# The keys' weight scale ahead of the second row tile's preparation, seven warming products fewer, and two stretches of the execution order rewritten

## The chip, the cores and the metric

The kernel runs on one core of one Trainium2 chip. The metric is the device time of one execution in microseconds (us), as the median of several runs. In what follows PE is TensorE, DVE is VectorE, ACT is ScalarE, POOL is GpSimd and SP is SyncE, the engine that issues nearly all transfers here.

## What is computed

```python
def _A_ref(x, wqkv, wo):                       # linear attention, 32 heads of 16
    qkv = (x @ wqkv).reshape(B, S, 3, H, Dh).transpose(2, 0, 3, 1, 4)
    q, k, v = qkv[0], qkv[1], qkv[2]
    phi = lambda t: where(t > 0, t + 1, exp(t)) + 1e-6
    pq, pk = phi(q), phi(k)
    kv = einsum("bhsd,bhse->bhde", pk, v);  z = einsum("bhsd->bhd", pk)
    num = einsum("bhqd,bhde->bhqe", pq, kv)
    den = einsum("bhqd,bhd->bhq", pq, z)[..., None] + 1e-6
    return (num / den).transpose(0, 2, 1, 3).reshape(B, S, D) @ wo
def _B_ref(x, w1, w3, w2):                     # SwiGLU
    return (silu(x @ w1) * (x @ w3)) @ w2

x = A_x                                        # 2048 rows of 512
for layer in range(2):                         # the same weights in both layers
    x = x + _A_ref(layernorm(x), wqkv, wo)
    x = x + _B_ref(layernorm(x), w1, w3, w2)   # inner width 1792
```

All is float32; one sequence of S = 2048 rows, D = 512.

## The kernel before

**Tiling.** The rows stand as 16 tiles of 128 (t = 0 to 15), D as four pieces of 128 (k). Each float32 matrix is split into a high and a low float16 part, and a product is made in three passes (high by high, low by high, high by low). Weights are scaled by a power of two ahead of the split, so that their largest value lies where float16 is finest.

**Stages.** Attention of layer 0 is plain (`attention`), tile by tile: keys, then queries, then output. The SwiGLU blocks and the attention of layer 1 (`attention7`) use a scheme with seven products instead of eight for pairs of halves; there the projections of queries and keys land in banks called qa, qb, qc, ka, kb, kc, and the SwiGLU's in ba, bb, bc. `po` is the bank of an output product.

**The lead-in** (lines 2328 to 2408). SP issues loads: x's first tile, four pieces of the keys' weights (`att_piece`), more tiles of x (`x_piece`, L2317), and blocks of the SwiGLU weights (`load_block`, L960, 896 KB each, b0, b1 and so on). For a tile of x, DVE takes the layer norm's moments (L907, L908), POOL makes scale and offset of them (L915 to L919), ACT normalises (L922). Tiles 0 and 1 are then turned on PE (`first_tile`): ACT rounds to the high half (L2356), POOL subtracts for the low half (L2358), PE multiplies four pieces of each half with an identity matrix (L2352, bank `turn`), ACT copies the turned halves out (L2354). Later tiles are turned by a transposing DMA (L937, L1856), with the split by L857 or L859 and L1855 before it.

In the same time the keys' weights are scaled and split: DVE takes the largest absolute value of each piece (L787), then of the four (L803), PE turns this column into a row (L806, bank `pm_k`), DVE takes the largest again (L808) and makes the scale (L809 to L819), and then ACT writes the high parts (L834) and DVE the low parts (L835), piece by piece. `keep_busy` (L2366) issues products of ones that nobody reads, so that PE works while it waits: 22 at the start and 10 behind `pm_k`.

**The key stage.** Tile by tile: twelve products `pk` on PE (L945), the positive map phi on ACT (L1337 to L1339) and DVE (L1348), the split of the result on ACT (L1394) and DVE (L1403), and then twelve products into `gt` (L945, four banks, the function `gram`), which use that split, two tiles behind.

**The order.** The program is emitted in the order of the Python code, and then `arrange` (L676) pins another order on each of the five engines: the table `ORDER` (L72 to L474) lists, for each engine, the instructions by their number in the order of emission, and each is chained behind the one ahead of it in the list. So an instruction can stand anywhere on its engine, as far as data and buffers allow, and what stands behind a waiting instruction waits too. Which piece of x or which block is issued when is decided by SP's list, not by the place of the call in the code. DVE's, ACT's and POOL's lists decide the same for the statistics, evictions and splits.

**The second layer's attention** runs at about 567 to 805 us of the profile. Query products land in qb, qc and qa; ACT empties them (L1632) or DVE does (L1636), and a bank is filled again only when it is empty. L1715, L1716, L1730 to L1751 and L1757, L1758 weigh the queries and divide; L1951 adds the output to x, POOL makes the next layer norm's scale (L1969, L1970), ACT normalises (L922) and splits (L1986), POOL subtracts (L1992), and the halves are turned by DMA.

Of the kernel before, what the change touches and what calls it, by code (L numbers as in the profile page):

```python
# [9 lines left out]
F32 = mybir.dt.float32  # L10
# [483 lines left out]
def kernel(  # L494
# [1833 lines left out]

    x_piece(0, 1)
    att_piece(1)  # L2330
    x_piece(1, 4)
    for item in LOADS[0].split():
        what, t = item.split(":")
        i = int(what[1:] or 0)
# [121 lines left out]
```

## Time and profile before

| | |
|---|---|
| median of 3 runs | 1139.43 us (1138.91 to 1141.31) |
| profiled execution, device time | 1139.86 us |
| span of its instructions | 1138.1 us |
| PE busy | 1125.6 us, 9124 products |
| DVE, ACT, POOL busy | 855.4, 661.2, 426.7 us |
| granted PE clock, mean of the span | 1.000 |
| data moved by DMA | 162.94 MB, mean 143 GB/s |

Times of events count from the span's start. A busy time of PE counts each product up to its modelled end, so products that run back to back overlap: a product of 512 columns has a busy time of 0.38 us, and the next one starts before it ends. Idle times of PE in the profile's brackets are therefore a little shorter than the distance of the starts tells.

### The profile page before, as it was taken

How to read it: one execution, taken by the hardware profiler on the slowest of the kernel's cores; microseconds unless marked ns; L12 is line 12 of the kernel's file. 1: busy time of each engine (PE TensorE's matmuls, PEld its weight loads, DVE VectorE, ACT ScalarE, POOL GpSimd, SP SyncE). 2: the span in 40 equal slices, each digit the busy share in tenths (PEclk: the TensorE clock that was granted, in tenths of full speed). 3: DMA queues.
4: the chain of work that ended last, by engine and by line, in shares of the span. 5: the costliest groups of instructions: out<-in, count | busy, mean ns of one | idle time of the engine just before them, and what ended most of it. 6: DMA issues, size and time to landing. Idle time of an engine off the chain costs nothing.

```text
span 1138.1 us, 22474 instructions
## 1 busy us (share of the span) xinstructions
PE 1125.6 (99%) x9124; PEld 888.9 (78%) x9124; DVE 855.4 (75%) x1468; ACT 661.2 (58%) x1104; POOL 426.7 (37%) x477
## 2 busy tenths in 40 slices
PE   8999999999999999999999999999999999999998
PEld 3445445888888888888886676578888888888887
DVE  6799878996978887889896488857855666465556
ACT  7678778765644455455578666586544434343442
POOL 5831697402001222344668416871152210302113
PEclk9999999999999999999999999999999999999999
DMA  8995765678573332241358955573372440220001
GB/s 255 281 305 182 175 139 111 146 224 239 171 257 141 117 149 102 92 174 66 80 130 187 267 207 124 112 170 69 98 215 87 178 190 1 84 84 29 11 20 56
DMA packets 171768, 162.94 MB, mean 143 GB/s; under 512 B 139536, under 2 KB 147984, under 8 KB 167056
## 3 DMA queue, kind: packets, MB, share of 16 engines
q1 hardware_dynamic: 171664, 161.51, 48.7%
q8 instruction: 71, 1.16, 0.4%
q14 instruction: 33, 0.27, 0.1%
HBM read 80.08 MB, written 47.32 MB: 112 GB/s over the span
## 4 chain that ended last, share of the span: by engine, by line
PE 90%; DVE 4%; POOL 3%; ACT 2%; DMA 1%; issue 1%; SPq 0%; POOLq 0%; ACTq 0%; DVEq 0%
PE bb L945 24%; PE po L2095 20%; PE bc L945 12%; PE gt L945 7%; PE ba L945 6%; PE po L945 4%; PE po L2115 3%; PE pq L945 3%; PE pk L945 3%; PE kb L945 2%; PE qb L945 1%; PE kc L945 1%; PE qc L945 1%; DMA arena<-in_A_x_dram 1%; DVE arena L869 1%
## 5 line engine op out<-in xcount | busy, mean ns | idle before, releaser
L945 PEld LDWEIGHTS <-arena 128*128 128x128 f16 x6648 | 646.1, 98 | 208.2 <-issue 7.3
L945 PE MATMUL bb<-arena 128*128 128x256 f16 x2688 | 350.1, 273 | 0.0
L2095 PE MATMUL po<-arena 128*128 128x256 f16 x2058 | 288.1, 273 | 0.0
L2050 ACT ACTIVATE arena<-bb 128x512 f32<-128x512 f32 x196 | 115.4, 594 | 200.3 <-PE bb L945 165.5
L2095 PEld LDWEIGHTS <-arena 128*128 128x128 f16 x2058 | 201.3, 98 | 23.5
L945 PE MATMUL bc<-arena 128*128 128x256 f16 x1344 | 179.5, 273 | 1.2 <-DVE arena L1951 1.1
L2053 DVE TENSOR_TENSOR arena<-arena,bc 128x512 f32<-128x512 f32 x112 | 76.6, 684 | 82.7 <-PE bc L945 48.6
L2005 ACT ACTIVATE arena<-arena,scalars 128x512 f32<-128x512 f32 x112 | 74.6, 666 | 88.9 <-DVE arena L2053 67.3
L2144 DVE SCALAR_TENSOR_TENSOR arena<-po,scalars,arena 128x256 f32<-128x256 f32 (+1 forms) x180 | 101.2, 584 | 31.1 <-PE po L2095 21.8
L2011 DVE TENSOR_TENSOR arena<-arena 128x1280 f16<-128x1280 f32 (+1 forms) x90 | 106.5, 1187 | 20.5 <-ACT arena L2009 20.2
L2009 ACT ACTIVATE arena<-arena 128x512 f16<-128x512 f32 (+1 forms) x112 | 101.1, 904 | 33.5 <-DVE arena L2024 13.4
L2006 DVE SCALAR_TENSOR_TENSOR arena<-arena,scalars 128x512 f32<-128x512 f32 x112 | 78.7, 706 | 38.1 <-ACT arena L2005 38.0
L945 PE MATMUL ba<-arena 128*128 128x256 f16 x672 | 91.8, 273 | 0.2 <-DVE arena L2006 0.2
L945 PE MATMUL gt<-arena 128*128 128x512 f16 x384 | 90.5, 379 | 1.3 <-DVE arena L1403 1.3
L945 PE MATMUL po<-arena 128*128 128x512 f16 x384 | 86.7, 379 | 1.6 <-DMA arena<-arena 1.6
L2011 POOL TENSOR_TENSOR arena<-arena 128x512 f16<-128x512 f32 x22 | 27.0, 1228 | 118.3 <-ACT arena L2009 111.3
L2153 POOL TENSOR_TENSOR arena<-arena 128x512 f32<-128x512 f32 x27 | 36.9, 1365 | 84.4 <-DVE arena L2144 84.4
L2152 POOL TENSOR_TENSOR arena<-arena 128x512 f32<-128x512 f32 x27 | 38.1, 1411 | 71.2 <-DVE arena L2144 69.1
L869 DVE SCALAR_TENSOR_TENSOR arena<-arena,scalars 128x512 f16<-128x512 f32 (+2 forms) x74 | 57.5, 792 | 2.5 <-ACT arena L867 2.4
L922 ACT ACTIVATE arena<-arena,nb_all,rs_all 128x512 f32<-128x512 f32 x64 | 50.6, 804 | 14.9 <-POOL nb_all L919 7.8
L2021 POOL TENSOR_TENSOR arena<-arena 128x256 f32<-128x256 f32 x10 | 7.8, 777 | 131.0 <-DVE arena L2006 131.0
L867 ACT ACTIVATE arena<-arena,scalars 128x512 f16<-128x512 f32 (+2 forms) x74 | 51.5, 717 | 6.2 <-DVE scalars L819 1.7
(234 smaller groups left out, 1458.1 us busy)
## 6 DMA issues: line engine op xcount, KB each, us to landing
arena<-xb_d SPq DMA_DIRECT2D x12, 1792.0 KB, 7.2
xb_d<-arena SPq DMA_DIRECT2D x8, 1792.0 KB, 7.4
w_d<-arena SPq DMA_DIRECT2D x5, 1792.0 KB, 7.7
arena<-w_d SPq DMA_DIRECT2D x5, 1792.0 KB, 8.0
arena<-in_B_w_dram SPq DMA_DIRECT2D x8, 896.0 KB, 7.0
arena<-in_B_w_dram SPq DMA_DIRECT2D x28, 256.0 KB, 3.0
xt_d<-arena SPq DMA_DIRECT2D x8, 896.0 KB, 4.5
arena<-xt_d SPq DMA_DIRECT2D x8, 896.0 KB, 5.4
```

What stands on the lines that cost most here:

```text
L867: nc.scalar.activation(hi, src, AF.Copy, scale=scale)
L869: lambda: nc.vector.scalar_tensor_tensor(lo, src, scale, hi, OP.mult, OP.subtract)
L922: nc.scalar.activation(dst, x_sb[:, t, :], AF.Identity, scale=rs_all[:, t : t + 1], bias=nb_all[:, t : t + 1],)
L945: nc.tensor.matmul(dst, lhs(a, k), rhs(b, k), start=first and k == 0 and i == 0, stop=last and k == n - 1 and i == len(PASSES) - 1, skip_g ...
L2005: nc.scalar.activation(t, gate, AF.Silu, scale=info["u1"])
L2006: nc.vector.scalar_tensor_tensor(t, up, info["hid"], t, OP.mult, OP.mult)
L2009: nc.scalar.activation(hs[:, 0, lo:hi], t[:, lo:hi], AF.Copy)
L2011: engine.tensor_tensor(hs[:, 1, lo:hi], t[:, lo:hi], hs[:, 0, lo:hi], OP.subtract)
L2050: nc.scalar.activation(dst, bank_, AF.Copy)
L2053: nc.vector.tensor_tensor(dst, dst, bank_, OP.add)
L2095: nc.tensor.matmul(po[:, i * HALF : (i + 1) * HALF], hs[:, a, qx, cs], w2[:, b, qw, :], start=g == ends[0] and i + a + b == 0, stop=g == e ...
L2144: nc.vector.scalar_tensor_tensor(dst, src, cb, to, OP.mult, OP.add)
```

## The change

The code of the lead-in is emitted in another order. Before: warming, statistics of tiles 0 and 1 (with two L787 and tile 0's preparation among them), tile 1's preparation, the weight scale (with tile 2's statistics and ten warming products inside), the split. After: warming, statistics of tile 0, all four L787, tile 0's preparation, the weight scale (with tile 1's statistics and three warming products inside), then tile 1's preparation, tile 2's statistics, the split. Since the pinned lists decide what runs when, this shifts the numbers in the lists; the lists themselves decide the rest.

```diff
-    x_piece(1, 4)
+    x_piece(1, 2)
+    x_piece(2, 4)
...
-    keep_busy(22)
-    ln_stats(0, 1)
-    parts = small.tile([P, NK], F32, tag="parts", name="parts")
-    ln_stats(1, 1)
-    abs_max(parts[:, 0:1], st_att[1][:, 0, :])
-    abs_max(parts[:, 1:2], st_att[1][:, 1, :])
-    first_tile(0)
-    for k in (2, 3):
-        abs_max(parts[:, k : k + 1], st_att[1][:, k, :])
-    first_tile(1)
-    issue_loads(1)
-    for i, _ in enumerate(weight_scale("k", parts, 2.0**14)):
-        if i == 0:
-            ln_stats(2, 1)
-        if i == 1:
-            keep_busy(10)
-    m, e, scale = info["k"]
...
+    if True:
+        keep_busy(22)
+        ln_stats(0, 1)
+        parts = small.tile([P, NK], F32, tag="parts", name="parts")
+        for k in range(NK):
+            abs_max(parts[:, k : k + 1], st_att[1][:, k, :])
+        first_tile(0)
+        for i, _ in enumerate(weight_scale("k", parts, 2.0**14)):
+            if i == 0:
+                ln_stats(1, 1)
+            if i == 1:
+                keep_busy(3)
+        first_tile(1)
+        issue_loads(1)
+        ln_stats(2, 1)
+        m, e, scale = info["k"]
...
```

The rest of that part (split, further factors, tile 2's preparation, tile 3's statistics) is the same, and `if True:` does nothing. The lists of `ORDER` are exchanged for others. Renumbered to the emission before, they are equal except in two stretches: from the start to about 128 us of the profile before, and from about 567 to 805 us. SP's list has the same numbering before and after; its beginning:

```diff
     "SP": (
-        "0 5-6 1 3 2 4 7 9-10 20 19 17 16 23 18 21 8 24 28 22 25 15 34 26 52 29 36 40 53 32 30 27 "
-        "39 41 35 33 43 57 42 11 48 47 37 31 50 38 46 51 55 45 44 71 56 58 49 59 14 60 54 61 65 "
...
+        "0 6 5 3 1 4 2 7 10 9 15 8 24 19 17 16 20 28 18 21-23 25 34 26 53 40 29 11 52 32-33 30 36 "
+        "27 39 41-42 35 47-48 57 46 51 37-38 50 43 55 45 58 56 44 59 31 49 61 60 65 54 63-64 62 "
...
```

Here 0, 5, 6, 7, 10, 9, 15, 8, 24, 19 and 28 are pieces of x (tiles 0, 1, 2, 3, 5, 4, 10, 7, 8, 6 and 9), 1 to 4 the keys' weights, 20 is the block b0, 31 and 49 the blocks b3 and b4, 54 and 65 two blocks more, 11 to 14 pieces of the values' weights and such, 60 and 63 the transposes of tiles 12 and 13.

What the lists say in names, for the places where the prediction looks (t0, t1, t2 are row tiles):

```
           before                                    after
SP         x0 x1 x2, keys' weights, x3               x0 x2 x1, keys' weights, x3
DVE        moments t0 t1 t2, 4 x L787, L803          moments t0 t1 t2, 4 x L787 (0,3,2,1), L803
POOL       identity; scale t0 t1 t2; L2358 t0, t1    scale t0; identity; scale t1 t2; L2358 t0, t1
ACT        cast of identity; L922 L2356 t0, t1;      L922 L2356 t0; L922 t1; cast of identity;
           L922 t2; copies t0; L935 t2; L834         L2356 t1; L922 L935 t2; copies t0; L834
           x 4; copies t1 high, low                  x 4; copies t1 low, high
PE         21 warm; turn t0 high, low, t1 high,      21 warm; turn t0 high and low by turns;
           low; one warm; pm_k; 10 warm; pk          pm_k; turn t1, with 4 warm among it; pk
ACT, 702   L1715, L1632 qc, L1632 qb, L922 x 2,      L1715, L1632 qc, L1632 qb, L1632 qb,
           L1986, L1632 qb, ...                      L922 x 2, L1986, ...
PE, 702    po t8, qb, qc, qb, qc, (the qb at         qb, qc, qb, po t8, qb, qc, (the qb at
           708.50), qb, qa, qb, qc, po               708.50), po, qa, qb, qb, po
```

SP's x pieces of tiles 10, 7 and 8 stand ahead of the block b0 after and behind the first transposes before; the block b3 stands directly ahead of b4 after, and some fifteen places earlier before. In the second stretch the loading of an activation table (in front of L1834) stands behind an L1757 at 730 us, and at 746 us before; some groups of `kb` products change places between 598 and 660 us.

More of the change, by code (lines that the diff above doesn't have):

```diff
@@ L2372, in keep_busy @@
             )
-    keep_busy(22)
-    ln_stats(0, 1)
-    parts = small.tile([P, NK], F32, tag="parts", name="parts")
-    ln_stats(1, 1)
-    abs_max(parts[:, 0:1], st_att[1][:, 0, :])
-    abs_max(parts[:, 1:2], st_att[1][:, 1, :])
-    first_tile(0)
-    for k in (2, 3):
-        abs_max(parts[:, k : k + 1], st_att[1][:, k, :])
-    first_tile(1)
-    issue_loads(1)
-    for i, _ in enumerate(weight_scale("k", parts, 2.0**14)):
-        if i == 0:
-            ln_stats(2, 1)
-        if i == 1:
-            keep_busy(10)
-    m, e, scale = info["k"]
-    for k in range(NK):
-        split(wk_s[:, 0, k, :], wk_s[:, 1, k, :], st_att[1][:, k, :], scale)
-    info["uk"] = scaled(e, 2.0**-23)
-    info["nuk"] = scaled(info["uk"], -1.0)
-    b = scalar()
-    nc.vector.tensor_scalar(b, m, float(D), 2.0, op0=OP.mult, op1=OP.add)
-    low_pow2(b, b)
-    nc.vector.reciprocal(b, b)
-    info["tk"] = scaled(b, 2.0**14)
-    info["itk"] = scalar()
-    nc.vector.reciprocal(info["itk"], info["tk"])
-    first_tile(2)
-    ln_stats(3, 1)
+    if True:
[14 more added lines that the diff above has]
+        m, e, scale = info["k"]
+        for k in range(NK):
+            split(wk_s[:, 0, k, :], wk_s[:, 1, k, :], st_att[1][:, k, :], scale)
+        info["uk"] = scaled(e, 2.0**-23)
+        info["nuk"] = scaled(info["uk"], -1.0)
+        b = scalar()
+        nc.vector.tensor_scalar(b, m, float(D), 2.0, op0=OP.mult, op1=OP.add)
+        low_pow2(b, b)
+        nc.vector.reciprocal(b, b)
+        info["tk"] = scaled(b, 2.0**14)
+        info["itk"] = scalar()
+        nc.vector.reciprocal(info["itk"], info["tk"])
+        first_tile(2)
+        ln_stats(3, 1)
     for t in range(3):
```

725 rows, old and new, of the table ORDER are left out of this document.

## The prediction

> **What bounds the kernel now.** I read the page first: busy times, slices, chain.
>
> ```profile
> PE 1125.6 (99%) x9124; PEld 888.9 (78%) x9124; DVE 855.4 (75%) x1468; ACT 661.2 (58%) x1104; POOL 426.7 (37%) x477
> ...
> PEclk9999999999999999999999999999999999999999
> ...
> PE 90%; DVE 4%; POOL 3%; ACT 2%; DMA 1%; issue 1%; SPq 0%; POOLq 0%; ACTq 0%; DVEq 0%
> ```
>
> TensorE (PE) works 1125.6 of 1138.1 us at full clock, and 90% of the chain is its products. No edit can bring more than the 12.5 us in which it stands, plus products left out. So the next view is that of the waits, for PE:
>
> ```profile
> PE turn L2352 <- POOL arena L2358: 2.0, 2, 1.4
> ...
> PE po L945 <- DMA arena<-arena: 1.6, 2, 0.8
> ...
> PE gt L945 <- DVE arena L1403: 1.3, 2, 0.7
> ...
> PE qb L945 <- ACT arena L1632: 1.0, 1, 1.0
> ```
>
> The columns are total, times and longest. Two waits lie in the lead-in (turn), two in the key stage of the first layer (gt); qb and po lie in the second layer's attention. All four are in the places where the change works; the question is which of them go, and what is late next. For that I went through the timeline of each place and set the old and the new hand-written order side by side.
>
> **The lead-in.** The rows of the timeline, up to the first key product:
>
> ```profile
> 1.11 6.70 PE L2366 MATMUL warm<-ones 128*128 128x512 f16 x21 [1.11 <-DVE ones L708]
> ...
> 4.32 0.66 DVE L907 BATCH_NORM_STATS2 st<-arena 128x6 f32<-128x512 f32 x1
> ...
> 5.83 0.69 DVE L907 BATCH_NORM_STATS2 st<-arena 128x6 f32<-128x512 f32 x1 [0.64 <-DMA arena<-in_A_x_dram]
> ...
> 6.66 2.68 DVE L787 TENSOR_REDUCE parts<-arena 128x1 f32<-128x512 f32 x4
> ...
> 6.90 0.19 POOL L915 TENSOR_SCALAR ve<-mv_all 128x1 f32<-128x1 f32 x1
> ...
> 8.23 2.27 POOL L2358 TENSOR_TENSOR arena<-arena 128x512 f16<-128x512 f32 x2
> ...
> 9.38 0.16 DVE L803 TENSOR_REDUCE scalars<-parts 128x1 f32<-128x4 f32 x1
> ...
> 9.44 0.51 PE L2352 MATMUL turn<-arena 128*128 128x128 f16 x6 [1.41 <-POOL arena L2358]
> ...
> 11.06 0.44 PE L806 MATMUL pm_k<-arena,scalars 128*128 128x128 f32 x2
> ...
> 11.34 2.32 PE L2366 MATMUL warm<-ones 128*128 128x512 f16 x10
> ...
> 13.19 2.74 DVE L835 SCALAR_TENSOR_TENSOR arena<-arena,scalars 128x512 f16<-128x512 f32 x4
> ...
> 13.55 0.81 PE L945 MATMUL pk<-arena 128*128 128x512 f16 x3
> ```
>
> The seven products that go would be 7 x 0.216 = 1.5 us (the ten take 2.32 us, of which the last one's own length, 0.38 by the page, so (2.32 - 0.38)/9 = 0.216 from start to start). But they are not what the first key products (pk) wait for in the end. Those need the four low parts of the keys' weights, which DVE writes from 13.19 to 15.93; the twelve products of tile 0 from 13.55 are done at 13.55 + 12 x 0.216 = 16.14. So the last of them starts just as the last low part is there. Without the seven, the products start earlier and wait in between. The price of the removal is nothing and so is its gain, unless the low parts come earlier. Do they?
>
> They hang on the scale: largest value (L787, L803), the turn on PE (pm_k), L808, exponent, split. The change gives x's third tile the second load, and on DVE the statistics of tile 1 still stand ahead of the four L787. Tile 1's statistics ran at 4.32, from the second transfer; now they need the third, which landed at 5.83. Then DVE does tile 1 and 2 in a row: 5.83 + two times about 0.8, so the four L787 start at about 7.5 and L803 ends at about 10.3 instead of 9.54. On POOL the scales of tiles 1 and 2 (each some 1.35 us, 6.90 to 8.23 in the rows) now both stand ahead of the first L2358: it starts at about 9.4 instead of 8.23, ends at 10.6, and PE gets its next product to turn at about 10.65 instead of 9.44. pm_k stands behind these turned products, eight of 0.06, so at 11.05 to 11.15: as before. ACT's two copies of tile 0's turned halves, which then stand right ahead of its high parts, end some 0.1 later than these began before (12.43). The low parts thus end at 15.95 to 16.05. Behind them ACT copies tile 1's turned halves in exchanged order (needed first, done last): another 0.1 to 0.3. Lead-in: +0.3 us, between 0 and +0.5; not the -1.5 that the count of products suggests.
>
> What the change opens is a gap on PE: the identity matrix that every turned product needs is built behind tile 0's scale on POOL and cast behind tile 1's normalising on ACT, so it is there at about 9.3 and not at 2.5. That itself delays nothing, for the low half comes at 10.6. But from 7.65, the end of the warming, to 10.65 PE has one product of 0.06: 2.9 us of standing, where before it stood 1.6 and then 0.8. The trace has only the other end: 21 warming products take 6.70 us, that is 11 x 0.216 + 10 x 0.43, so half speed for 4.3 us at the start, and after the gaps of 1.6 and 0.8 the ten run at 0.216. So 2.9 us of idling is between what was harmless and what is unseen. [...] No row of before shows a gap of this length. Its price is a rival below.
>
> **The key stage, 14 to 114 us.**
>
> ```profile
> 25.57 1.05 SPq L2317 DMA_DIRECT2D arena<-in_A_x_dram  x2
> ...
> 26.45 0.69 DVE L907 BATCH_NORM_STATS2 st<-arena 128x6 f32<-128x512 f32 x1 [1.31 <-DMA arena<-in_A_x_dram]
> ...
> 27.06 0.74 DVE L1403 SCALAR_TENSOR_TENSOR arena<-arena,scalars 128x512 f16<-128x512 f32 x1
> ...
> 27.85 2.32 PE L945 MATMUL gt<-arena 128*128 128x512 f16 x10 [0.71 <-DVE arena L1403]
> ...
> 40.21 0.68 DVE L907 BATCH_NORM_STATS2 st<-arena 128x6 f32<-128x512 f32 x1
> ...
> 40.82 0.73 DVE L1403 SCALAR_TENSOR_TENSOR arena<-arena,scalars 128x512 f16<-128x512 f32 x1
> ...
> 41.60 3.61 PE L945 MATMUL gt<-arena 128*128 128x512 f16 x16 [0.64 <-DVE arena L1403]
> ```
>
> The first gt wait: L1403 stood on DVE behind statistics that waited 1.31 us for a piece of x. In the new order of SP the x pieces 7, 8 and 10 are issued right after 5 and 4, some 15 to 20 us earlier, ahead of the weight block b0, and DVE does their statistics by about 24. Then the L1403 of tile 1 runs at about 26.5 and the stall goes: 0.87 us (product starts 0.216 apart; the last before it at 26.77). The second: L1403 of tile 3 and 4 come out at about 35.7 and 39.8 by the new order, wanted at 37.3 and 41.8; 0.80 us goes. Sum -1.67. I followed pk and gt so up to tile 9: slack 0.8 to 1.7 us each time, so nothing of DVE, ACT or POOL is late next.
>
> What is late next could be a transpose. The window table and SP's row:
>
> ```profile
> 60.00:80.00 20.00, 20.00 (x96) 9.46 (x95) 18.19 (x34) 14.58 (x24) 6.47 (x10) 1.00 1.12 316
> ...
> 80.00:100.00 20.00, 20.00 (x95) 9.56 (x94) 19.56 (x45) 15.45 (x27) 0.56 (x4) 1.00 0.49 148
> ...
> 47.79 0.44 SPq L960 DMA_DIRECT2D arena<-in_B_w_dram  x1
> ...
> 62.92 2.09 SPq L1856 DMA_TRANSPOSE arena<-arena  x1
> ...
> 68.27 3.93 SPq L1856 DMA_TRANSPOSE arena<-arena  x1
> ...
> DMA to landing us min/median/max: 7.1/7.1/7.1
> ...
> 72.04 2.75 PE L945 MATMUL pk<-arena 128*128 128x512 f16 x12
> ```
>
> (In the first two rows the last columns are DMA share and GB/s, and the fifth is DVE's busy time; the landing row is that of the transpose issued at 62.92.) From 60 to 80 the transfers are full: share 1.12. Tile 12's transpose, issued at 62.92, landed at 70.0, and its pk began at 72.04. The change moves the block b3 (896 KB, issued at 47.79) to just before b4, close ahead of this transpose, and takes a 256 KB piece out from in front. PE wants tile 12 at about 69.5. If the DMA stays as full in 45 to 60, the backlog ahead of the transpose is no larger and it lands before that: no cost. If the time that b3 leaves is not filled, 0.9 MB at 316 GB/s, 2.9 us, comes on top of 70.0: 3.4 us of stall. The earlier issue (tile 12's preparation moves with PE) takes some 1.5 off. I take +0.3, nearer the first, since the wo pieces and stores move into that place; the ends are 0 and 3.4. From 80 to 100 DVE is busy 19.56 of 20: work that the new order pushes out of the earlier stretch finds 0.44 us there. The stalls at 114.4 and later begin from PE's own ends and shift with it.
>
> **The second layer's attention, 567 to 805 us.**
>
> ```profile
> 702.08 1.13 ACT L1715 ACTIVATE arena<-arena,scalars 128x1024 f32<-128x1024 f32 x1
> ...
> 705.82 1.52 ACT L922 ACTIVATE arena<-arena,nb_all,rs_all 128x512 f32<-128x512 f32 x2 [1.71 <-POOL nb_all L1970]
> ...
> 707.91 0.55 ACT L1632 ACTIVATE arena<-qb,ones,scalars 128x256 f32<-128x256 f32 x1
> ...
> 708.50 1.47 PE L945 MATMUL qb<-arena 128*128 128x256 f16 x12 [0.99 <-ACT arena L1632]
> ...
> 733.18 4.32 POOL arena L1992 x3
> ...
> 742.55 4.08 DMA arena<-arena
> ...
> 746.67 2.76 PE L945 MATMUL po<-arena 128*128 128x512 f16 x12 [0.83 <-DMA arena<-arena]
> ```
>
> At 708.50 PE waits for a bank that ACT's L1632 empties at 707.91. That L1632 stands behind two L922, and these behind POOL (ACT idles 1.71). The new order puts it ahead of them, into the idle time. The stall (1.15 us) and two small ones behind it (0.16, 0.18) go: -1.5. In exchange PE's qc group now comes before the eviction behind L1715 (702.08 to 703.2): about +0.9 there by hand, part of which the moved qb and po products take. PE is then some 0.5 ahead at 715. The chain that decides at 746.67 (DVE L1636, L1716, POOL L1758, L1992 x3, transposes, po) starts from qb evictions that come about 1.1 earlier, so both po stalls (736.56 and 746.67) stay and what is behind them moves by -1.15. The kb products moved at 598 to 660 meet six stalls of 0.13 to 0.20: -0.3 (0 to -0.5). The load of an activation table, moved from 746 to 730 on ACT, falls into idle time there; uncovered it costs 1.3. Stretch: -1.45, between 0 and -2.3.
>
> **Sum.** 0.3 - 1.67 + 0.3 - 1.45 = -2.5 us against the profiled execution's 1139.86: 1137.3. The median of the runs (1139.43) lies 0.43 below that execution, so 1136.9. A measurement here tells 0.2% from nothing, 2.28 us: the forecast lies just beyond that bound.
>
> **Rivals.**
>
> 1. Transposes late, slower. Tile 12's lands 3.4 late, and tile 13's (issued at 68.27 before, now also behind b5 and another block) 1.5 to 2; DVE, full from 80, can't give it back. +0.3 - 1.67 + 5.2 - 1.45 = +2.4: 1141.8. It decides from the point at which tile 12 lands after 72: then its stall alone (2.5) outweighs what the stage gained. For it: the share of 1.12. Against: the bytes ahead of the transpose are fewer by 256 KB. Chance 0.22.
> 2. The clock falls in the 2.9 us gap. Then some 4.3 us of products at half speed follow, ten of 512 columns, 0.21 more each: +2.1, sum -0.4: 1139.0. For it: fewer products behind the gap. Against: gaps of 1.6 and 0.8 did nothing. Chance 0.08.
> 3. The warming products did hold pk (ten end at 13.66, pk begins at 13.55): lead-in -1.5 instead of +0.3, sum -4.3: 1135.1. Against: the low parts' end at 15.93. Chance 0.10.
> 4. The second stretch does nothing: the wait at qc and a longer one at 746.67 take all of it: sum -1.1: 1138.3. For it: both po stalls hang on transposes and POOL, not on PE. Chance 0.10.
>
> **The numbers.** The forecast has 0.50. Around it the spread is some 1.5 us, from the ends of the two unsure terms: 0.32 of it is faster by over 0.2%, 0.16 within, 0.02 slower. Rival 1 gives 0.20 slower and 0.02 within; rival 2 0.05 within, 0.01 faster, 0.02 slower; rival 3 0.10 faster; rival 4 0.10 within. Faster 0.43, within 0.2% 0.33, slower 0.24. Range 1134.4 to 1142.0: below it lies about a tenth (rival 3 with a good second stretch), above it about a tenth (rival 1 with more than its price).
>
> **What would show it.** Right: tile 0's last pk ends at 16.2 to 16.5, the pm_k product runs near 11.1, the gt waits for L1403 are gone, no qb wait for L1632 near 708, po still waits for transposes near 735 and 745. Wrong: a pk that waits for a DMA between 65 and 82 (rival 1); products of 512 columns 0.43 apart after 10.6 (rival 2); a tile 0 done before 15 (rival 3); the po wait of 0.83 grown to 2 (rival 4).

## The result, and the profile after

| | before | changed |
|---|---|---|
| median of 22 runs each | 1139.93 us | 1137.41 us |
| profiled execution, and its span | 1139.86, 1138.1 us | 1137.83, 1136.1 us |
| products on PE | 9124 | 9117 |
| mean granted clock of the profiled execution | 1.000 | 0.998 |

The ratio is 0.9977, 95% interval 0.9970 to 0.9983: faster by 2.5 us. The forecast was 1136.9 us within 1134.4 to 1142.0, a gain of 2.5. The total came out as forecast; the terms for the lead-in and for the second stretch did not, and two waits that the sum left out went as well.

In what follows, line numbers of the changed kernel stand one or two higher than before (L2366 is L2368, L945 is L946, L1632 is L1633). First the view of PE's waits, after:

```profile
PE turn L2354 <- ACT arena L705: 1.7, 1, 1.7
PE qb L946 <- ACT arena L1633: 1.3, 1, 1.3
PE turn L2354 <- POOL arena L2360: 1.2, 1, 1.2
...
PE kc L946 <- DMA arena<-arena: 0.4, 1, 0.4
PE turn L2354 <- DVE scalars L809: 0.4, 1, 0.4
PE qc L946 <- ACT arena L1633: 0.3, 1, 0.3
```

Both gt waits for L1403 are gone, and both po waits. The turn waits have become longer (2.9 us, and 0.4 more, instead of 2.0), a qb wait for the same line is there at another place, and kc and qc wait where they did not. Counted from start to start of its products, PE stands (or runs at half clock) for 13.8 us before and 13.3 after; with the seven products that is the 2.0 us of the spans.

Since both programs issue the same products behind the lead-in, the start of the n-th product from the end can be set against that of the same n in the trace of before. The difference (minus: ahead of before) at several places, in us, worked out from the traces of single executions:

| time in the trace of before | 24 | 45 | 128 | 230 to 560 | 640 | 700 | 780 to the end |
|---|---|---|---|---|---|---|---|
| changed | +1.11 | -0.55 | -0.85 | -1.18 | -0.52 | -0.48 | -2.02 |
| first stretch alone | +0.68 | -0.99 | -1.28 | -1.61 | -1.17 | -1.19 | -1.98 |
| second stretch alone | +0.24 | +0.37 | +0.37 | +0.36 | +0.40 | +0.45 | -0.51 |
| gap filled | -0.03 | -1.03 | -1.32 | -1.65 | -1.42 | -1.37 | -2.58 |
| ten warming products | +1.94 | +0.28 | -0.02 | -0.34 | -0.20 | -0.15 | -0.68 |
| before, three warming products | +0.01 | -0.09 | -0.08 | -0.07 | +0.26 | +0.25 | -0.59 |
| before, x early | +1.90 | +0.23 | +0.24 | +0.24 | +0.39 | +0.39 | +0.14 |
| x's tile 1 second | -0.57 | -1.59 | -1.88 | -2.20 | -1.52 | -1.47 | -2.99 |
| qb first | +0.42 | -1.24 | -1.54 | -1.86 | -1.20 | -1.16 | -2.38 |
| gap filled, block behind | +0.18 | -0.30 | -0.60 | -0.92 | -0.88 | -0.75 | -1.84 |
| gap filled, block behind, x's tile 1 second | -0.28 | -1.94 | -2.24 | -2.56 | -2.51 | -2.45 | -3.76 |
| changed, once more | +1.63 | -0.04 | -0.33 | -0.66 | +0.99 | +1.03 | -0.46 |
| gap filled, once more | -0.11 | -1.77 | -2.07 | -2.39 | -2.19 | -2.14 | -3.64 |

The first row is the result in short: the lead-in costs 1.11, the first stretch gives back 2.29, the second brings another 0.84. The other rows are the experiments below. A second trace of the changed kernel has +1.63, -2.29 and +0.20 in the same places: the first stretch repeats, the other two differ from execution to execution.

The lead-in after, PE and DVE from the timeline:

```profile
5.94 0.70 DVE L908 BATCH_NORM_STATS2 st<-arena 128x6 f32<-128x512 f32 x1 [1.72 <-DMA arena<-in_A_x_dram]
...
7.57 2.49 DVE L788 TENSOR_REDUCE parts<-arena 128x1 f32<-128x512 f32 x4
...
9.29 0.22 PE L2354 MATMUL turn<-arena 128*128 128x128 f16 x1 [1.69 <-ACT arena L705]
...
10.68 0.56 PE L2354 MATMUL turn<-arena 128*128 128x128 f16 x7 [1.17 <-POOL arena L2360]
...
11.08 0.44 PE L807 MATMUL pm_k<-arena,scalars 128*128 128x128 f32 x2
...
12.60 1.06 PE L2368 MATMUL warm<-ones 128*128 128x512 f16 x2
...
13.20 2.74 DVE L836 SCALAR_TENSOR_TENSOR arena<-arena,scalars 128x512 f16<-128x512 f32 x4
...
14.41 2.84 PE L946 MATMUL pk<-arena 128*128 128x512 f16 x11
```

The statistics of tile 1 wait for the third transfer, the identity is there at 9.29, the low half at 10.68, pm_k at 11.08, and the low parts run from 13.20 to 15.94, as in the kernel before. All of that stands in the prediction within 0.1 us. But the two warming products at 12.60 take 1.06 us, where two at full clock take 0.59 (0.22 and 0.38). The first key product starts at 14.41 instead of 13.55; it waits for the slow products ahead of it on PE, not yet for low parts. The windows of the two kernels say it directly; the third figure from the end is the clock that was granted. Before:

```profile
7.00:12.00 5.00, 2.98 (x26) 1.80 (x25) 3.54 (x8) 3.89 (x7) 4.05 (x8) 1.00 1.02 396
12.00:15.00 3.00, 3.00 (x16) 1.41 (x15) 2.97 (x13) 2.57 (x5) 1.19 (x3) 1.00 0.86 247
```

After:

```profile
7.00:12.00 5.00, 1.76 (x15) 0.97 (x14) 4.19 (x11) 3.86 (x8) 4.60 (x11) 0.96 1.03 392
12.00:15.00 3.00, 3.00 (x14) 1.62 (x14) 2.92 (x11) 2.86 (x6) 1.58 (x3) 0.50 0.71 204
```

PE is at half clock from 12 to 15 us (by the trace's record of the clock from 11.6 to 15.0): the second rival, which had a chance of 0.08, is what this execution shows.

The key stage after, DVE's L1404 (L1403 before) for tiles 1, 2, 3 and 4:

```profile
25.61 0.75 DVE L1404 SCALAR_TENSOR_TENSOR arena<-arena,scalars 128x512 f16<-128x512 f32 x1 [1.45 <-ACT arena L1395]
...
30.38 0.75 DVE L1404 SCALAR_TENSOR_TENSOR arena<-arena,scalars 128x512 f16<-128x512 f32 x1 [0.43 <-ACT arena L1395]
...
35.48 0.73 DVE L1404 SCALAR_TENSOR_TENSOR arena<-arena,scalars 128x512 f16<-128x512 f32 x1
...
39.61 0.77 DVE L1404 SCALAR_TENSOR_TENSOR arena<-arena,scalars 128x512 f16<-128x512 f32 x1 [1.77 <-ACT arena L1395]
```

No PE wait is between 15 and 188 us. The transposes of tiles 11 to 15 (all those issued from 55 to 85 us), from issue to landing:

```profile
DMA to landing us min/median/max: 3.0/3.8/4.5
```

Tile 12's took 7.1 before and takes 3.8 here; b3 and b4 ahead of it did not make it late. And the second layer's attention after, PE from the timeline:

```profile
634.73 0.83 PE L946 MATMUL kc<-arena 128*128 128x256 f16 x6 [0.44 <-DMA arena<-arena]
...
702.94 0.81 PE L946 MATMUL qc<-arena 128*128 128x256 f16 x6 [0.30 <-ACT arena L1633]
...
713.47 1.47 PE L946 MATMUL qb<-arena 128*128 128x256 f16 x12 [1.26 <-ACT arena L1633]
...
725.34 15.87 PE L946 MATMUL po<-arena 128*128 128x512 f16 x72
```

Counted from start to start PE stands 0.61, 0.47 and 1.43 us ahead of the first three. The po products run through in one piece where they stood for 0.8 us, and the next ones, at 745, did not wait either.

### The profile page after: what moved, and what is told of

It is laid out like the page before. It is cut to its first block, busy times and chain, and to the rows that moved or that the text cites. A ratio compares the mean times of both kernels' runs of the same rounds, so it can differ in the third digit from the quotient of the medians.

```text
span 1136.1 us, 22462 instructions
## 1 busy us (share of the span) xinstructions
PE 1124.7 (99%) x9117; PEld 887.9 (78%) x9117; DVE 853.9 (75%) x1468; ACT 660.7 (58%) x1104; POOL 427.9 (38%) x477
## 3 DMA queue, kind: packets, MB, share of 16 engines
q8 instruction: 71, 1.16, 0.4%
## 4 chain that ended last, share of the span: by engine, by line
PE 94%; DVE 2%; POOL 2%; DMA 1%; issue 1%; ACT 0%; SPq 0%; POOLq 0%; DVEq 0%; ACTq 0%
PE bb L946 26%; PE po L2096 20%; PE bc L946 13%; PE gt L946 7%; PE ba L946 6%; PE po L946 5%; PE pk L946 4%; PE pq L946 3%; PE po L2116 3%; PE kb L946 2%; PE qb L946 1%; PE kc L946 1%; PE qc L946 1%; PE kv L946 0%; DMA arena<-arena 0%
## 5 line engine op out<-in xcount | busy, mean ns | idle before, releaser
L946 PEld LDWEIGHTS <-arena 128*128 128x128 f16 x6648 | 645.7, 98 | 205.8 <-issue 6.2
L946 PE MATMUL bb<-arena 128*128 128x256 f16 x2688 | 350.2, 273 | 0.0
L946 PE MATMUL bc<-arena 128*128 128x256 f16 x1344 | 179.4, 273 | 1.1 <-DVE arena L1952 1.1
L946 PE MATMUL ba<-arena 128*128 128x256 f16 x672 | 91.8, 273 | 0.0
L946 PE MATMUL gt<-arena 128*128 128x512 f16 x384 | 89.9, 379 | 0.0
L946 PE MATMUL po<-arena 128*128 128x512 f16 x384 | 86.9, 379 | 0.0
L923 ACT ACTIVATE arena<-arena,nb_all,rs_all 128x512 f32<-128x512 f32 x64 | 50.4, 805 | 11.3 <-POOL nb_all L920 6.3
```

Of the source, the lines that this page charges most:

```text
L923: nc.scalar.activation(dst, x_sb[:, t, :], AF.Identity, scale=rs_all[:, t : t + 1], bias=nb_all[:, t : t + 1],)
L946: nc.tensor.matmul(dst, lhs(a, k), rhs(b, k), start=first and k == 0 and i == 0, stop=last and k == n - 1 and i == len(PASSES) - 1, skip_g ...
```

## The experiments

**The stretches apart.** The first kernel takes the changed lists up to about 300 us and those of before behind, the second the other way round.

```diff
 ORDER, all five lists, renumbered
-  start to 128 us new, 567 to 805 us new
+  e1: start to 128 us new, 567 to 805 us as before
+  e2: start to 128 us as before, 567 to 805 us new
```

> The changed kernel's lead-in and first stretch, with the order of before from about 300 us on. Theory (the two stretches act by themselves): in the traces PE is 1.18 us ahead at 300 us and stays so until 567, so the time is 1.2 us under before, ratio 0.9990, and the waits behind 567 us are those of before, the qb wait of 1.15 near 707 among them. Rival (the second stretch's waits hang on chains that do not start from PE's ends): they take back what PE is ahead, and less than 0.6 us is left, ratio 0.9995 or more.

Measured: 1137.55 us, ratio 0.9978 (0.9968 to 0.9987). In its trace PE is 1.61 us ahead at 560 and 1.98 at the end. Not less, as the rival had it, but more than the theory: nearly all of the result. At 560 it is 0.43 more than the changed kernel's 1.18, just what this execution's lead-in cost less (0.68 instead of 1.11).

> The kernel before up to about 400 us, the changed order behind. Theory (the stretches act by themselves): -0.84 us, ratio 0.9993, with the new waits of the changed trace, kc for a transpose (0.6) near 636 and qb for ACT's L1632 (1.4) near 715. Rival (the kc wait is there only because PE comes 1.2 us earlier in the changed kernel): without it -1.45 us, ratio 0.9987.

Measured: 1140.1 us, ratio 1.0002 (0.9993 to 1.0011). In the trace -0.87 from 560 us to the end, as in the changed kernel (-0.84), but without the kc wait and with a po wait of 0.60 near 746 in its place; the median shows nothing of it. The rival's condition was met, for the kc wait was gone, but not its gain of 1.45. Single executions differ in this stretch: with the old order the four traces (before, the first stretch alone, and the two kernels made from the one before below) give 0, -0.37, -0.52 and -0.10 from 560 us on, mean -0.25; with the new order nine (that of the qb wait below left out) give from +0.20 to -1.25, mean -0.77. By the traces the second stretch is worth about 0.5 us; no median confirms it.

**The gap in the lead-in.** Twelve warming products more, behind the first 21:

```diff
-        keep_busy(22)
+        keep_busy(34)
...
     "PE": (
-        "0-20 22 26 23 27-28 24-25 29-30 34 38 21 39 31-32 35-37 40-41 33 42-65 78-89 66-77 "
+        "0-32 34 38 35 39-40 36-37 41-42 46 50 33 51 43-44 47-49 52-53 45 54-77 90-101 78-89 "
```

> The changed kernel with twelve warming products more, right behind the first 21, where PE stands from 7.6 to 9.3 and to 10.7 us: 12 x 0.216 = 2.6 us of them. Theory (it was the gap that sent the clock to half from 11.9 to 15.1 us, and that made the first key product late): the products behind pm_k run 0.216 apart, tile 0's keys end at about 16.2 instead of 17.3, and the time is 1.0 us under the changed kernel's, ratio to before 0.997 - 0.001 = 0.9968. Rival (the keys wait for the low parts or the turned halves, and the clock adds nothing): the clock stays up, but tile 0's keys still end after 17, and the time is that of the changed kernel, 0.9977.

Measured: 1136.51 us, ratio 0.9967 (0.9954 to 0.9980), clock 1.000 in each of its five executions. The same two windows:

```profile
7.00:12.00 5.00, 4.27 (x28) 2.31 (x27) 3.73 (x9) 4.30 (x8) 4.68 (x9) 1.00 1.02 388
12.00:15.00 3.00, 2.80 (x18) 1.30 (x17) 2.93 (x10) 2.60 (x5) 0.86 (x3) 1.00 1.00 228
```

The lead-in costs -0.03 instead of +1.11. It was the gap. Tile 0's keys end at 16.2 us, where they ended at 17.3 in the changed kernel. Of the 1.14 us, 0.6 is left at the end, since a key product now waits:

```profile
21.77 0.42 SPq L961 DMA_DIRECT2D arena<-in_B_w_dram  x1
...
22.92 1.25 SPq L1857 DMA_TRANSPOSE arena<-arena  x1
...
29.77 1.47 PE L946 MATMUL pk<-arena 128*128 128x512 f16 x6 [0.50 <-DMA arena<-arena]
```

That is the first rival's mechanism (a transpose behind a weight block) at tile 4, not 12: 6.8 us from 22.92 to its landing. In the second trace of the same program, the last run below, this transpose landed after 5.2 us and nothing waited.

**The seven products put back**, right behind pm_k (PE's list has them there):

```diff
-                keep_busy(3)
+                keep_busy(10)
```

> The changed kernel with its seven warming products put back right behind pm_k, at 11.3 us. Theory (the gap ahead of pm_k has decided by then): the clock falls at about 11.9 all the same, the seven run 0.43 apart, 3.0 us of which about 1 falls into PE's waits, so the first key product comes 1.5 to 2 us later than in the changed kernel: 1.5 to 2 us above it, ratio to before 0.9990 to 0.9995. Rival (the seven products that are missing sent the clock down): it stays up, and tile 0's keys end at about 16.2 as in the kernel before: 1.0 us under the changed kernel, ratio 0.9968.

Measured: 1138.98 us, ratio 0.9982 (0.9973 to 0.9991), and the lead-in costs 1.94 in the trace. In that execution the clock falls at 11.0, behind the gap, although the ten products stand there, and each of the seven then costs 0.43:

```profile
7.00:12.00 5.00, 2.17 (x15) 1.16 (x14) 4.24 (x14) 4.35 (x8) 4.68 (x10) 0.90 1.04 386
12.00:15.00 3.00, 3.00 (x12) 1.28 (x11) 2.95 (x10) 2.56 (x4) 1.27 (x3) 0.60 0.79 218
```

The theory holds for this execution: the seven that are missing did not send the clock down, and they make the fall dearer. The median is lower than expected, because not every execution lost its clock: of the eleven five have a mean clock of 0.998 (mean 1139.15), one 0.999 and five 1.000 (1137.26).

**Only the seven products left out, in the kernel before:**

```diff
-            keep_busy(10)
+            keep_busy(3)
```

> The kernel before with three warming products behind pm_k instead of ten, nothing else. Theory (the low parts of the keys' weights set the end of tile 0, and the standing of 1.6 and 0.8 us ahead does not cost the clock): tile 0's keys end at 16.1 to 16.3 as before, and the time is the same, ratio 1.0000. Rival A (the ten products held the keys): tile 0's keys end at about 14.8, 1.3 to 1.5 us less, ratio 0.9987. Rival B (the seven were what kept the clock): products of 512 columns 0.43 apart after 12 us and a time 1 us longer, ratio 1.0009.

Measured: 1140.23 us, ratio 1.0000 (0.9992 to 1.0009). From PE's timeline:

```profile
11.35 0.81 PE L2366 MATMUL warm<-ones 128*128 128x512 f16 x3
...
13.21 0.59 PE L945 MATMUL pk<-arena 128*128 128x512 f16 x2 [1.00 <-ACT arena L834]
14.00 7.54 PE L945 MATMUL pk<-arena 128*128 128x512 f16 x34 [0.20 <-DVE arena L835]
```

PE stands 1.16 us for the high part and 0.36 for a low part, 1.5 together, just the time of the seven; at 16 us it is where it was (+0.01). They covered a wait and were worth nothing.

**Only three loads of x moved, in the kernel before:**

```diff
     "SP": (
-        "0 5-6 1 3 2 4 7 9-10 20 19 17 16 23 18 21 8 24 28 22 25 15 34 26 52 29 36 40 53 32 30 27 "
+        "0 5-6 1 3 2 4 7 9-10 15 8 24 20 19 17 16 23 18 21 28 22 25 34 26 52 29 36 40 53 32 30 27 "
```

> The kernel before with one change: on SP the pieces of x for tiles 10, 7 and 8 stand right behind those of tiles 4 and 5, ahead of the block b0. Theory (the first gt wait comes from DVE's statistics that wait for these pieces, the second from the order of DVE's list): the wait of 0.87 near 27.9 us goes, that of 0.80 near 41.6 stays, -0.87 us, ratio 0.9992. Rival A: both go, -1.67 us, ratio 0.9985. Rival B (the blocks and transposes that now come behind the pieces are late instead): ratio 1.0000 or more, with a pk or gt wait for a transfer.

Measured: 1138.73 us, ratio 0.9987 (0.9978 to 0.9996). Both gt waits went, 1.66 us from 24 to 45 us in the trace: rival A, not the theory. One line of one list gives the whole of the first stretch's two stalls, -1.3 us by the medians. The profiled execution itself is a long one, because the lead-in cost 1.90 there: PE stood 2.1 us for POOL, and the windows show

```profile
7.00:12.00 5.00, 2.38 (x20) 1.49 (x19) 3.48 (x7) 3.93 (x7) 3.88 (x8) 0.90 1.05 394
12.00:15.00 3.00, 3.00 (x10) 1.22 (x10) 2.49 (x13) 1.67 (x3) 1.45 (x3) 0.60 1.00 400
```

So the lead-in of the kernel before can lose its clock too.

**Tile 1 of x second again:**

```diff
     "SP": (
-        "0 6 5 3 1 4 2 7 10 9 15 8 24 19 17 16 20 28 18 21-23 25 34 26 53 40 29 11 52 32-33 30 36 "
+        "0 5-6 3 1 4 2 7 10 9 15 8 24 19 17 16 20 28 18 21-23 25 34 26 53 40 29 11 52 32-33 30 36 "
```

> The changed kernel with x's pieces of tiles 1 and 2 in their old order on SP, so that tile 1's statistics need the second transfer again. Theory (its statistics, which wait for the third transfer, hold the scale and POOL's first low half): statistics of tile 1 at about 4.3 instead of 6.8, the largest values from 6.7 instead of 7.6, POOL's first low half at about 8.5 instead of 9.5; the standing of PE behind the warming is 2 us instead of 2.9, the clock stays up, and tile 0's keys end 1 to 2 us earlier than in the changed kernel: ratio to before 0.9977 - 0.0010 to 0.0018, 0.9959 to 0.9967. Rival (the next transposes or the clock bind all the same): less than 0.5 us under the changed kernel.

Measured: 1137.43 us, ratio 0.9972 (0.9961 to 0.9983). In the trace tile 0's keys come 1.7 us earlier than in the changed kernel and the clock stays up, as the theory has it. The largest values are there only 0.2 us earlier, for DVE now waits for the weights (L788 at 7.08 and 7.99); what comes earlier is pm_k, at 10.49 instead of 11.08, behind POOL's low half. Of the 1.7 us, 0.64 is lost to tile 4's transpose at 29.2. But the median is that of the changed kernel: three of the seven executions have a mean clock of 0.998. The step is right for an execution that keeps its clock, and the gain is not shown.

**The qb wait at 713.5.** ACT's list, the eviction 738 ahead of the L923 772:

```diff
-        "727-728 736 757 756 764 729-730 772 765 738 731 766 773 737 746 741 747 742 739 748 740 "
+        "727-728 736 757 756 764 729-730 738 772 765 731 766 773 737 746 741 747 742 739 748 740 "
```

> The changed kernel with one ACT instruction moved: the L1633 that empties the qb bank for which PE waits 1.43 us at 713.5 stands right behind the L1716 of 708.3, ahead of the L923 that waits for POOL until 711.85. Theory (the wait was an order of ACT, and the transposes behind it have slack): the wait goes and what is behind it moves by 1 us or more: ratio to before 0.9977 - 0.0009 = 0.9968 or less. Rival (POOL's chain and the transposes end last in this stretch): the po products near 735 and 745 wait instead, as in the kernel before (1.0 each), and less than 0.4 us is gained.

Measured: 1137.42 us, ratio 0.9978 (0.9968 to 0.9988). PE from the timeline:

```profile
711.36 1.47 PE L946 MATMUL qb<-arena 128*128 128x256 f16 x12
...
712.67 2.75 PE L946 MATMUL po<-arena 128*128 128x512 f16 x12
...
716.43 0.82 PE L946 MATMUL qb<-arena 128*128 128x256 f16 x6 [1.01 <-DVE arena L1637]
...
717.49 1.47 PE L946 MATMUL qc<-arena 128*128 128x256 f16 x12 [0.25 <-DVE arena L1637]
```

The wait at 713 went, and three others took its place, 1.17, 0.41 and 0.23 us between 716 and 720. Set against the changed kernel's trace it gains 1.4 us from 709 to 716 and has lost 1.7 again by 746. Neither outcome named for the place is right (po did not wait), but the rival's point is: the chain beside PE, POOL's L1759 and L1752 and what ACT and DVE do behind them, ends last there, and nothing is gained.

**The block behind the transpose, and all of it together.** On the kernel with the gap filled, b1 behind tile 4's transpose; then tile 1 of x second as well, with ten products in the gap:

```diff
     "SP": (
-        "0 6 5 3 1 4 2 7 10 9 15 8 24 19 17 16 20 28 18 21-23 25 34 26 53 40 29 11 52 32-33 30 36 "
+        "0 6 5 3 1 4 2 7 10 9 15 8 24 19 17 16 20 28 18 21-22 25 23 34 26 53 40 29 11 52 32-33 30 "
```

> The changed kernel with the gap filled (twelve warming products more, as in the run with the gap filled) and with the weight block b1, which stands directly ahead of tile 4's transpose on SP, put behind it. In the run with the gap filled that transpose took 6.8 us from issue to landing and the keys of that tile waited 0.66 us at 29.8. Theory (the block ahead of the transpose is what makes it late): the wait goes, 0.6 us under the run with the gap filled, ratio to before 0.9967 - 0.0005 = 0.9962. Rival (the transfers are full there whatever the order, and the next one is late instead): a wait of a later key product for a transfer, or the b1 block late, and no gain.

Measured: 1136.43 us, ratio 0.9972 (0.9962 to 0.9983): no gain over the filled gap that could be told. The transpose landed 3.0 us after its issue, and the wait at 29.8 went; two came one tile later, 0.70 and 0.47 us:

```profile
33.05 1.67 PE L946 MATMUL gt<-arena 128*128 128x512 f16 x7 [0.54 <-DVE arena L1404]
...
35.02 1.25 PE L946 MATMUL pk<-arena 128*128 128x512 f16 x5 [0.30 <-DMA arena<-arena]
```

In the two traces with b1 behind the transpose it took 3.0 and 3.1 us, in the eight with b1 directly ahead of it 4.4 to 6.9: the block makes it slower, but not always so late that the keys wait.

> The same (here ten warming products fill the gap) with x's pieces of tiles 1 and 2 in their old order as well. Theory (with the clock up in every execution, the earlier scale of tile 1 gives its full -0.55 us, which the run with the old order of the pieces showed in its profile): tile 0's keys end at about 15.6, another 0.5 us less, ratio to before 0.9957. Rival (the first transposes, which do not come earlier, take it back): a wait for a transfer by 30 us, and the same time as without it, 0.9962.

Measured: 1136.8 us, ratio 0.9972 (0.9961 to 0.9982). Its profiled execution is the shortest of all that were profiled (span 1134.4 us, against 1134.5 in the second trace of the filled gap alone); the median of its eight is not lower than that of the filled gap alone.

**The changed kernel and the filled gap once more, on one chip.**

> The changed kernel itself, on the same chip as the next run. Theory (in some executions the standing ahead of pm_k sends the clock to half for 3 us, in others not): two groups of executions, at a mean clock of 0.998 and at 1.000, about 1.1 us apart, more than half of them in the slower one as in the 22 executions of the result. Rival (the 1.1 us are something of the chip that ran them): one group.

Measured: 1138.1 us, ratio 0.9976 (0.9967 to 0.9985). Of its eleven executions five have a mean clock of 0.998 (mean time 1138.04), one 0.999, five 1.000 (1137.65): 0.4 us apart. The execution at 0.999 (1139.41) is the profiled one, and its trace has the fall too: a fall in the lead-in takes 1.71 us of full clock, 0.0015 of the span, so it can show as 0.998 or as 0.999. Without a fall in the lead-in a mean of 0.999 comes about as well, from a fall behind the last product (up to 0.9 us of clock in the traces). With the profiled execution counted in, the groups are 0.6 apart. Of the 22 of the result thirteen have 0.998 (1137.86), two 0.999 and seven 1.000 (1136.76): 1.1 apart. Two groups, but how far apart is not settled by these.

> The changed kernel with the gap filled by twelve warming products, on the same chip as the run ahead. Theory: no execution under a clock of 1.000, and a time equal to the faster group of the changed kernel, 0.5 to 0.7 us under its median. Rival (no gain from the gap): the same median.

Measured: 1136.61 us, ratio 0.9967 (0.9955 to 0.998), 1.5 us under the changed kernel on the same chip. That is also 1.0 under the faster group there (1137.65), which it was expected to equal: on this chip the mean clock accounts for about 0.5 of the 1.5, and where the rest comes from is open. With the gap filled, in three kernels and 25 executions, none has a mean clock of 0.998; in the changed kernel 18 of 33 have it, in the kernel before 23 of the 80 that ran beside the experiments. The filled gap has the lowest ratio of all, 0.9967 of the kernel before in both of its runs, against 0.9977 and 0.9976 of the changed one, with intervals that overlap.

## Why the prediction was right, and where it was not

1. **The seven warming products are worth nothing.** Right, and shown by taking out only these: ratio 1.0000, with PE standing 1.5 us in their place. The third rival (they held the keys) fell.
2. **The lead-in, +0.3.** Its steps were right to 0.1 us, from the statistics at 5.94 to the low parts' end at 15.94. The term was mis-sized: +1.11 in the profiled execution, because the step that called 2.9 us of standing "between what was harmless and what is unseen" gave the fall of the clock a chance of 0.08; that was the author's estimate, for no row of before has a gap as long. The fall came in more than half of the executions (18 of the 33 of the changed kernel have a mean clock of 0.998). Two signs named in the prediction speak for the second rival: products of 512 columns 0.43 apart, and tile 0's keys ending at 17.3 instead of 16.2 to 16.5. The rival's price was right in kind and too high: the lead-in costs 0.42, 0.68, 1.11 and 1.63 us in the four traces of it with a fall, not 2.1 more, for the clock was down for 3.4 us, not 4.3, and in part of these PE would have waited for the low parts anyway. With the gap filled and the clock up it costs -0.11, -0.03 and +0.18 in three traces.
3. **The two gt waits, -1.67.** Right: -1.66 from 24 to 45 us. L1404 of tiles 3 and 4 began at 35.5 and 39.6, where 35.7 and 39.8 were worked out, and that of tile 1 ran from 25.6 to 26.4, where 26.5 was. What the prediction did not see is that the three loads alone do it.
4. **The stalls at 114 and 207 us shift with PE.** Wrong: both went, 0.29 and 0.33 us. They stay in the kernel before with x early and go with the first stretch alone, so they belong to the lists, not to the loads. With the gt waits they make up the first stretch's -2.29. At 204 us two L2005 of ACT, and at 180 a few instructions of DVE, have changed places, so the lists differ there too, and not only in the two stretches that the account of the change names. Which entry did it was not tried.
5. **Tile 12's transpose, +0.3 of 0 to 3.4.** The near end was right: it landed 3.8 us after its issue at 64.0, and no key product waited. The slower rival fell for tile 12; its mechanism cost 0.6 us at tile 4 in two traces with an early lead-in (gap filled, x's tile 1 second), and nothing in the second trace of the filled gap.
6. **The second stretch, -1.45.** The wait at 708 went, as said. The step that failed is what is late next: not 0.9 at qc with both po waits staying, but 0.47 at qc, 1.43 at a qb 5 us later and 0.61 at a kc for a transpose, with both po waits gone. It came to -0.84 in the trace and to about -0.5 over nine traces against four. The waits for transposes do not belong to the new order: a kc wait is there with the old order too (first stretch alone; three warming products), and a po wait of 0.8 with the new one (ten warming products). In the two traces of the new order in which nothing in this stretch waits for a transfer, it gives -1.25 and -1.20, near the -1.45.
7. **The sum.** +1.11 - 2.29 - 0.84 = -2.02 in the profiled execution, against +0.3 - 1.67 + 0.3 - 1.45 = -2.5. The clock cost 0.8 more, the first stretch brought 0.9 more, the second 0.6 less. That the total agrees with the forecast is luck as far as these cancel: 0.8 lost to the clock against 0.9 from waits that were not in the sum. The gt waits alone came as forecast.

## What to carry to other kernels

Here the products that only keep PE busy cost nothing where they cover a wait for an operand, and nothing was gained by taking seven of them out (ratio 1.0000): look for the operand that ends last. In the gap, where PE would stand, ten or twelve of them went with a kept clock (no mean of 0.998 in 25 executions, against 18 of 33 without them), so look at how long an engine stands and at the clock that was granted. A wait that a new order removes can come back at the next chain that has not moved (1.15 us at 708 went, 1.43 us at 713 came), so the second wait has to be priced in the same view; and the stretches of a change should be run apart, and traced more than once, since a sum can be right by chance. A load that a busy engine's list waits for, ahead of work that others need, was cheap to move: three entries of one list gave half of this change (1.3 of 2.5 us by the medians).

## What the runs showed of the hardware

PE's clock fell in the lead-in, to which the prediction gave a chance of 0.08. Counted by the starts of its products, PE stood 1.85 and 1.33 us in the changed kernel with one small product between, and was at half clock from 11.6 to 15.0 us. With x early it stood 2.1 and 0.8 us with 0.35 us of work between them, and the clock fell as well (mean 0.90 from 7 to 12 us, 0.60 from 12 to 15); in the profiled execution of before it stood 1.6 and 0.8, and the clock stayed at 1.00.

Set side by side, the fourteen traces show what goes with the fall. By their record of the granted clock, full clock first comes 3.8 to 6.6 us into the span; until then the warming products start 0.43 us apart. In six traces (the changed kernel twice, the first stretch alone, ten warming products, x early, qb first) the clock fell 6.83 us after that, and it stayed down for 3.41. In the last 3.41 us ahead of the fall PE was busy for 0.6 to 1.1 us. In the other eight traces the clock stayed up; in these, with the time from full clock on counted in lengths of 3.41 us, PE was busy for at least 1.9 us in each of the first four. What lies between 1.1 and 1.9 us no run shows, nor whether another way of counting would tell the traces apart as well.

The time at which full clock came differs between executions of the same program: 4.76 us in one trace of the changed kernel and 4.84 in the other, 4.65 and 5.73 in the two with the gap filled. So does the fall: 18 of the 33 executions of the changed kernel have a mean clock of 0.998, twelve have 1.000, and the gap has a chance as well as a price. That the one decides the other was not shown.
